# Two tiles of the last phase in two buffers each, two small tiles in another tile's buffers

## The chip, the cores and the metric

The kernel runs on one core of a Trainium2 chip. The metric is the device time of one execution in microseconds (us); lower is better. Engine names follow the profile: PE is the matmul engine, PEld its weight loads, DVE the vector engine, ACT the scalar engine, POOL GpSimd, SP the engine that issues almost all DMAs, SPq its queue.

## The reference

The program computes the forward result and all gradients of `out = x + A(LN(x)) + B(LN(x))`, with S = 2048 rows and D = 512 columns, in bf16. LN is a layer norm without weights.

```python
# A: gated long convolution
k_shift = sum_t k_pad[:, t:t+S] * shift_k[:, 3-t]        # 4 taps
kv = k_shift * v
y  = irfft(rfft(kv, 2S) * rfft(ssm_k, 2S))[:S] + kv * ssm_D
A  = xn * y                                              # xn = LN(x)
# B: bilinear GLU, F = 1376
B  = ((xn @ w_gate) * (xn @ w_up)) @ w_down
out = x + A + B
# returned: out (out_0) and the gradients for x, k, v, shift_k, ssm_k, ssm_D, w_gate, w_up, w_down
```

With `go` the gradient that comes in and `bb` the two parts that the GLU contributes to a block of rows (`x + B(xn)` and the GLU's gradient for `xn`), the element-wise end of it is, per block of rows:

```
out_0 = xn * y + bb[0]
e     = go * y ;  dxn = e + bb[1]
out_1 = go + rstd * (dxn - mean(dxn) - xn * mean(dxn * xn))     # gradient for x (the q gradient)
out_2 = four taps of (dks * shift_k), summed                     # gradient for k
```

## The kernel before

Rows are dealt as `s = 16 p + r`: partition `p` holds rows 16 p to 16 p + 15, so a tile `[128, 16, 512]` holds a whole sequence tensor, and a block `b` is the two columns of rows `2 b` and `2 b + 1`, a tile of `[128, 2, 512]` (256 KB in bf16). The FFT is done as matmuls in two stages with the spectra in DRAM in between.

The program has a first part (layer norm, FFT stages, the GLU's forward and backward pass over 8 chunks of rows) that leaves its results in DRAM scratch: `BX` (the `bb` parts), `HDD` (hidden gradients), `GD` (inverse spectra). The last phase, from about 314 us on, is where the change lies. Its main line is the generator `dw()` (weight gradients): for each of 11 blocks of the hidden dimension it loads `hb` from `HDD` (or, for the last three, `natT`, turned by the DMA), transposes it on PE (`hid_t`), multiplies it with `goC` (`down_grad`, line 1014, tile `pd`, stored by way of `od`) and with `xnC` (line 1050, tile `pu`, stored by way of `og`). At each `yield` of `dw()`, counted by `n`, a list of side generators may be advanced:

- `inv_y()`: last stage of the inverse FFT, in 8 steps. Spectra come in as `g` (line 785); the rows of `y` go to `yC`, the convolution's other gradient to tiles `dd`, from which DVE makes rows of `dks` (line 950) and `kb` (line 951, stored as out_3). For this it loads `vb` and `kb` (lines 925, 927).
- `dsk_gram()`: the gradient of `shift_k`, from `n` = 27 on. Four PSUM tiles `pk` (line 1073) are masked into `kd` (line 1079) and reduced into `dsk` (line 1081); then a transposed copy `dskt` (line 1091) is stored as out_4.
- `inv_dk()`: the gradient of `ssm_k` (tiles `po`, `o5t`).
- `ew()`: the element-wise end, one step every third `n` from `n` = 10 on. Its steps are `final(0)`, `final(1)`, `bwd(0)`, `final(2)`, `bwd(1)`, ... `final(7)`, `bwd(6)`, `bwd(7)`. `final(b)` asks for the next block's `bb` (line 1114) and computes `o` (out_0; lines 1125 and 1126) and `e` (out_1; lines 1129, 1134, 1140, 1141). `bwd(b)` computes `dk` (out_2; lines 1103 to 1106) with a helper tile `tk`. Stores are not issued where a tile is finished: they are put on a list, and `put_late()` (line 1167) issues them on SP at the start of the next step.

The order of each engine's instructions is fixed at build time. A planner goes through the traced program, and on each engine takes, of the instructions that it holds to be ready, the one traced earliest; `tc.high_priority(offset=SOON)` moves an instruction forward in that order, `tc.issue_after(ins)` keeps one behind another. On the chip every engine and SP's queue then run strictly in that order, and semaphores hold an instruction back until its inputs are there and the buffer it writes is free. A DMA that waits on SP therefore holds everything behind it on SP.

Tiles come from pools. A pool has a default number of buffers per tile name; tiles with the same `tag` share buffers. The pools of the last phase are `c2b` (two buffers: `vb`, `kb`, `dd`, `dk`, `bb`, `od`) and `c2` (one buffer: `yC`, `dks`, `o0`, `e`, `dxn`, `kd`, `dskt`, `og`, `khC` and others). In the profile `o0` appears as `o`. The hidden dimension's last `og` tile (`og1`) already sits in the buffers of `dd`. `tk` shares the one buffer of `dxn`.

Of the kernel before, what the change touches and what calls it, by code (L numbers as in the profile page):

```python
# [8 lines left out]
BF = mybir.dt.bfloat16  # L9
F32 = mybir.dt.float32  # L10
# [8 lines left out]
D = 512  # L19
F = 1376  # L20
R = 16
P = 128
NC4 = 4
# [167 lines left out]
def kernel(  # L191
# [45 lines left out]
    def dve(o, i):  # L237
        nc.vector.tensor_copy(o, i)  # L238
# [13 lines left out]
    def P2(name, shape, dt=F32):  # L252
        return ps2.tile(shape, dt, name=name, tag="p2")

    def P1(name, shape, dt=F32):
        return ps1.tile(shape, dt, name=name, tag="p1")
# [648 lines left out]
    c2b = ctx.enter_context(tc.tile_pool(name="c2b", bufs=2, side="right", reuse_waits="tile"))  # L905
    c2 = ctx.enter_context(tc.tile_pool(name="c2", bufs=1, side="right", reuse_waits="tile"))
# [160 lines left out]
    def dsk_gram():  # L1067
        for c in range(NC4):
            pk = P2("pk", [P, 2, D])
            for r in range(R):  # L1070
                for h in range(2):
                    c0 = c * 128 + 64 * h
                    nc.tensor.matmul(pk[64 * h:64 * h + 64, h, 0:256], lhsT=dks[:, r, c0:c0 + 64],  # L1073
                                     rhs=KH[0][:, r:r + 4, c0:c0 + 64], start=(r == 0), stop=(r == R - 1))
            kd = c2.tile([P, 4, 64], F32, name="kd")
            with tc.high_priority(offset=SOON):
                for h in range(2):
                    hs = slice(64 * h, 64 * h + 64)
                    nc.vector.tensor_tensor(kd[hs], pk[hs, h, 0:256].rearrange("q (j c) -> q j c", j=4),
                                            ident[hs, hs].unsqueeze(1).to_broadcast((64, 4, 64)), op=ALU.mult)  # L1080
                nc.vector.tensor_reduce(dsk[:, c, :], kd[:], axis=AX.X, op=ALU.add)
            yield
        dskb = c2.tile([P, 4, NC4], BF, name="dskb")
        nc.vector.tensor_copy(dskb[:], dsk[:].rearrange("q c i -> q i c"))
        for _ in range(2):
            yield
        pt = P1("pts", [P, 4, P], BF)
        for j in range(4):
            nc.tensor.transpose(pt[:NC4, j, :], dskb[:, 3 - j, :], ident[:])
        dskt = c2.tile([NC4, P, 4], BF, name="dskt")  # L1090
        dve(dskt[:], pt[:NC4].rearrange("c j q -> c q j"))
        nc.sync.dma_start(out_4.rearrange("(c p) j -> c p j", p=128), dskt[:])
        yield
# [18 lines left out]
    def load_fin(b):  # L1112
        bb = c2b.tile([P, 2, 2, D], BF, name="bb")
        nc.sync.dma_start(bb[:], BX[:, 2 * b:2 * b + 2, :, :])
        FL[b] = bb

    def final(b):
        if b + 1 < 8:
            load_fin(b + 1)
        bb = FL.pop(b)  # L1120
        rb = slice(2 * b, 2 * b + 2)
        tt = nc.vector.tensor_tensor
        stt = nc.vector.scalar_tensor_tensor
        o = c2.tile([P, 2, D], BF, name="o0")
        tt(o[:], xnC[:, rb], yC[:, rb], op=ALU.mult)
        tt(o[:], o[:], bb[:, :, 0, :], op=ALU.add)
        late.append((o0_n[:, rb, :], o))
        e = c2.tile([P, 2, D], BF, name="e")
        tt(e[:], goC[:, rb], yC[:, rb], op=ALU.mult)
        dxn = c2.tile([P, 2, D], F32, name="dxn")  # L1130
        for i in range(2):
            r = 2 * b + i
            stt(dxn[:, i], e[:, i], 1.0, bb[:, i, 1, :], op0=ALU.mult, op1=ALU.add, accum_out=s1[:, r:r + 1])
            stt(e[:, i], dxn[:, i], 1.0, xnC[:, r, :], op0=ALU.mult, op1=ALU.mult, accum_out=s2[:, r:r + 1])
        nc.vector.tensor_scalar(m2[:, rb], s2[:, rb], -1.0 / D, None, op0=ALU.mult)
        stt(m1[:, rb], s1[:, rb], -1.0 / D, rstd[:, rb], op0=ALU.mult, op1=ALU.mult)
        for i in range(2):
            r = 2 * b + i
            stt(dxn[:, i], xnC[:, r, :], m2[:, r:r + 1], dxn[:, i], op0=ALU.mult, op1=ALU.add)
            nc.vector.tensor_scalar(e[:, i], dxn[:, i], rstd[:, r:r + 1], m1[:, r:r + 1], op0=ALU.mult, op1=ALU.add)  # L1140
        tt(e[:], e[:], goC[:, rb], op=ALU.add)
        late.append((o1_n[:, rb, :], e))
# [16 lines left out]
    for b in range(8):  # L1159
        tail.append(lambda b=b: final(b))  # L1160
        if b > 0:
            tail.append(lambda b=b: bwd(b - 1))
# [19 lines left out]
    def load_dk():  # L1182
        gks.append(load_gk(0))
        gks.append(load_gk(1))
        yield

    sides = [every(seq(inv_y(), load_dk()), 0, 3), every(dsk_gram(), 27, 2), every(inv_dk(), 35, 3), every(ew(), 10, 3)]
    for n, _ in enumerate(dw()):
        for sd in sides:
# [36 lines left out]
```

## Time and profile before

| | us |
|---|---|
| runs (median of 3; lowest; highest) | 489.96; 488.36; 490.24 |
| the profiled execution | 488.56 |
| its span, first to last instruction | 486.8 |
| last phase: end of the last matmul | 477.08 |
| last phase: end of DVE's last instruction | 481.35 |
| DVE busy in 300 to 487 us | 113.96 of 187 |
| PE busy in 300 to 477 us | all but 0.2 |

A page of the profile gives, for one execution, the busy time of each engine, the idle time ahead of each group of instructions with what ended it, and the chain of work that ended last. In a timeline line the columns are start in us, duration in us, engine, line, operation, tiles and shape, count, and in square brackets the idle time just ahead and what released it. In the list of waits they are the total in us, the number of waits and the longest.

### The profile page before, as it was taken

The numbers are of one execution on the slowest core, as the hardware profiler recorded it, in microseconds if no ns is written. First come the engines' busy times: TensorE is split into PE (matmuls) and PEld (weight loads), VectorE is DVE, ScalarE is ACT, GpSimd is POOL, SyncE is SP. The second block draws the span as 40 slices with busy tenths as digits, with TensorE's granted clock in tenths as the row PEclk, the third lists the DMA queues.
The fourth block names the chain that finished last, engine by engine and source line by source line (L and its number), as shares of the span: only waits on it lengthen the run. The fifth ranks groups of instructions, "written<-read, shape, count | busy, mean of one in ns | idle before, by whom it ended". The sixth has DMA issues, their size and how long they took to land.

```text
span 486.8 us, 10509 instructions
## 1 busy us (share of the span) xinstructions
PE 471.5 (97%) x4335; PEld 314.8 (65%) x4335; DVE 342.0 (70%) x625; ACT 310.1 (64%) x351; POOL 13.9 (3%) x30
## 2 busy tenths in 40 slices
PE   8998999999999999999999999999999999999992
PEld 7867755547647457357357734577677778777790
DVE  7889989988275667677687874021260999998895
ACT  4956677669568678789689954567557523733320
POOL 8000000000000000000000000020000000000000
PEclk9999999999999999999999999999999999999997
DMA  8999999889999978788977199989999797999518
GB/s 266 373 366 362 314 261 359 295 314 323 306 293 284 247 235 246 240 257 250 296 231 238 63 366 324 369 314 348 342 368 373 286 354 248 316 310 231 186 48 293
DMA packets 105837, 139.87 MB, mean 287 GB/s; under 512 B 33435, under 2 KB 78912, under 8 KB 104126
## 3 DMA queue, kind: packets, MB, share of 16 engines
q1 hardware_dynamic: 104206, 137.85, 86.9%
q10 hardware_dynamic: 1584, 1.36, 1.0%
q8 instruction: 34, 0.56, 0.5%
q14 instruction: 13, 0.11, 0.1%
HBM read 68.45 MB, written 63.41 MB: 271 GB/s over the span
## 4 chain that ended last, share of the span: by engine, by line
PE 76%; DMA 11%; DVE 10%; ACT 1%; issue 1%; DVEq 0%; SPq 0%; ACTq 0%
PE px L555 14%; PE pgu L512 13%; PE pu L1050 12%; PE py L548 7%; PE pd L1014 6%; PE pdh L518 6%; PE pt L847 4%; PE pq L920 3%; PE ps L584 3%; DMA ssk<-in_A_ssm_k_dram 3%; PE pg L613 3%; PE pf L370 2%; DMA out_dram<-e 2%; DMA x_b<-in_A_q_dram 2%; PE pk L1073 2%; DMA XN<-x_b 1%
## 5 line engine op out<-in xcount | busy, mean ns | idle before, releaser
L555 PE MATMUL px<-WT,hd 128*128 128x512 bf16 (+1 forms) x352 | 81.0, 380 | 0.0
L1050 PEld LDWEIGHTS <-xnC 128*128 128x128 bf16 x704 | 67.1, 98 | 8.8 <-issue 0.9
L555 PEld LDWEIGHTS <-hd 128*128 128x128 bf16 (+1 forms) x352 | 32.8, 98 | 44.4 <-issue 7.7
L1050 PE MATMUL pu<-natd,xnC 128*128 128x256 bf16 x512 | 58.5, 273 | 0.2 <-ACT nath L235 0.2
L235 ACT CAST gu<-pgu 128x1024 bf16<-128x1024 f32 (+1 forms) x48 | 45.4, 946 | 16.5 <-PE pgu L512 16.3
L235 ACT CAST GO<-pg 128x1024 bf16<-128x1024 f32 x48 | 46.2, 1015 | 13.8 <-issue 7.2
L235 ACT CAST SP<-ps 128x1024 bf16<-128x1024 f32 x47 | 45.6, 1025 | 13.7 <-PE ps L584 11.8
L600 DVE TENSOR_TENSOR T<-SP 128x2048 bf16<-128x2048 bf16 x24 | 29.4, 1223 | 34.8 <-ACT SP L235 34.7
L512 PE MATMUL pgu<-xt,Wu 128*128 128x256 bf16 (+1 forms) x352 | 53.1, 273 | 0.7 <-DVE kn L238 0.6
L512 PE MATMUL pgu<-xt,Wg 128*128 128x256 bf16 (+1 forms) x352 | 52.8, 273 | 0.2 <-DMA Wg<-in_B_w_gate_dram 0.2
L518 PE MATMUL pdh<-gt,WdT 128*128 128x256 bf16 (+1 forms) x352 | 46.9, 273 | 0.2 <-ACT WdT L235 0.2
L235 ACT CAST fst<-pf 128x1024 bf16<-128x1024 f32 x44 | 42.7, 1030 | 5.7 <-ACT fst L235 2.1
L512 PEld LDWEIGHTS <-Wu 128*128 128x128 bf16 (+1 forms) x352 | 33.0, 100 | 15.0 <-issue 10.1
L548 PE MATMUL py<-Wd,hd 128*128 128x512 bf16 (+1 forms) x176 | 41.4, 380 | 0.0
L235 ACT COPY natd<-pt 128x2048 bf16<-128x2048 bf16 x16 | 30.0, 1874 | 14.1 <-PE pt L847 14.1
L235 ACT CAST og<-pu 128x1024 bf16<-128x1024 f32 (+1 forms) x11 | 10.9, 993 | 43.1 <-PE pu L1050 38.5
L518 PEld LDWEIGHTS <-WdT 128*128 128x128 bf16 (+1 forms) x352 | 34.8, 100 | 5.0 <-ACT WdT L235 0.4
L512 PEld LDWEIGHTS <-Wg 128*128 128x128 bf16 (+1 forms) x352 | 34.8, 100 | 4.1 <-DMA Wg<-in_B_w_gate_dram 0.5
L533 DVE TENSOR_TENSOR hd<-gu,dh 128x1024 bf16<-128x1024 bf16 (+1 forms) x48 | 30.9, 643 | 0.8
L532 DVE TENSOR_TENSOR hd<-gu 128x512 bf16<-128x512 bf16 (+1 forms) x48 | 19.1, 398 | 15.9 <-ACT gu L235 15.9
L1014 PE MATMUL pd<-goC,nath 128*128 128x512 bf16 x128 | 30.1, 379 | 0.0
L548 PEld LDWEIGHTS <-hd 128*128 128x128 bf16 (+1 forms) x176 | 16.5, 98 | 20.8 <-issue 3.1
(176 smaller groups left out, 693.2 us busy)
## 6 DMA issues: line engine op xcount, KB each, us to landing
HDD<-hd SPq DMA_DIRECT2D x35, 384.0 KB, 5.8
FD<-fst SPq DMA_DIRECT2D x24, 512.0 KB, 5.5
X<-FD SPq DMA_DIRECT2D x24, 512.0 KB, 5.2
GD<-GO SPq DMA_DIRECT2D x24, 512.0 KB, 3.9
g<-GD SPq DMA_DIRECT2D x11, 1024.0 KB, 8.7
hb<-HDD SPq DMA_DIRECT2D x8, 1344.0 KB, 7.9
bb<-BX SPq DMA_DIRECT2D x8, 512.0 KB, 6.2
BX<-bx SPq DMA_DIRECT2D x7, 512.0 KB, 3.9
```

Source lines behind the costliest of these rows:

```text
L235: nc.scalar.copy(o, i)
L512: nc.tensor.matmul(pgu[:w, i, t, :], lhsT=W[:, c, f0:f0 + w], rhs=xt[:, :, c, :], start=(c == 0), stop=(c == NC4 - 1))
L518: nc.tensor.matmul(pdh[:w, i, :], lhsT=WdT[:, c, f0:f0 + w], rhs=gt[:, :, c, :], start=(c == 0), stop=(c == NC4 - 1))
L532: nc.vector.tensor_tensor(hd[:fw, fb0:fb0 + n, 0, :], gu[:fw, :n, 0, :], gu[:fw, :n, 1, :], op=ALU.mult)
L533: nc.vector.tensor_tensor(hd[:fw, fb0:fb0 + n, 1:3, :], gu[:fw, :n], dh[:fw, :n].unsqueeze(2).to_broadcast((fw, n, 2, 256)), op=ALU.mult)
L548: nc.tensor.matmul(py[:], lhsT=hd[:fw, fb, 0, ss], rhs=Wd[:fw, fb, :], start=(fb == 0), stop=(fb == NFB - 1))
L555: nc.tensor.matmul(px[:], lhsT=hd[:fw, fb, t, ss], rhs=W[:fw, fb, :], start=(t == 1 and fb == 0), stop=(t == 2 and fb == NFB - 1))
L584: nc.tensor.matmul(ps[32 * q:32 * q + 32, a, :], lhsT=TB.EF[64 * a:64 * a + 64, 4 * g + q, ri].rearrange("p k j -> p (k j)"), rhs=X[64 * a ...
L600: tt(W[:].rearrange("p c a d -> p c (a d)"), A[:, i:i + 1].rearrange("p c a d -> p c (a d)").to_broadcast((P, 2, 2 * D)), B[:].rearrange(" ...
L847: nc.tensor.transpose(pt[:, r, :fw], hs[:, (r % 2) * 128:(r % 2) * 128 + 128], ident[:fw, :fw])
L1014: nc.tensor.matmul(pd[:fw, :], lhsT=nat_h(fb, r), rhs=goC[:, r, :], start=(r == 0), stop=(r == R - 1))
L1050: nc.tensor.matmul(pu[:, c, :, :fw], lhsT=xnC[:, r, cs(c)], rhs=nat_d(fb, r), start=(r == 0), stop=(r == R - 1))
```

## The change

`o` and `e` in `final()` get two buffers each, so that a block's tile can be written while the tile of the block before is still being stored. `kd` and `dskt` of `dsk_gram()` move from pool `c2` (one buffer each) into the two buffers of `dd` in pool `c2b`, which `inv_y()` has done with by then and `og1` takes later. No computation and no DMA is added or taken away. In bytes per partition `c2` loses 1024 for `kd` and 1024 for `dskt` and gains 2048 each for `o` and `e`; the buffers of `dd` (2048 each) keep their size.

```diff
@@ dsk_gram()
-            kd = c2.tile([P, 4, 64], F32, name="kd")
+            kd = c2b.tile([P, 4, 64], F32, name="kd", tag="dd")
...
-        dskt = c2.tile([NC4, P, 4], BF, name="dskt")
+        dskt = c2b.tile([NC4, P, 4], BF, name="dskt", tag="dd")
@@ final(b)
-        o = c2.tile([P, 2, D], BF, name="o0")
+        o = c2.tile([P, 2, D], BF, name="o0", bufs=2)
         tt(o[:], xnC[:, rb], yC[:, rb], op=ALU.mult)
         tt(o[:], o[:], bb[:, :, 0, :], op=ALU.add)
         late.append((o0_n[:, rb, :], o))
-        e = c2.tile([P, 2, D], BF, name="e")
+        e = c2.tile([P, 2, D], BF, name="e", bufs=2)
```

## The prediction

> **What bounds the kernel now.** I read the page's busy times first, then busy time by stretch for the end of the run.
>
> ```profile
> PE 471.5 (97%) x4335; PEld 314.8 (65%) x4335; DVE 342.0 (70%) x625; ACT 310.1 (64%) x351; POOL 13.9 (3%) x30
> 448.62:477.08 28.46, 28.46 (x276) 23.48 (x273) 23.77 (x50) 7.77 (x10) 0.00 (x0) 1.00 0.47 154
> 477.08:486.80 9.72, 0.01 (x1) 0.00 (x0) 4.10 (x7) 0.37 (x1) 0.00 (x0) 0.73 0.85 268
> ```
>
> The last two lines give a stretch, its length, and the busy time of PE, PEld, DVE, ACT and POOL, then PE's granted clock, DMA share and GB/s. PE has no gap up to 477.08 and nothing after it. So the end of the run is 477.08, set by PE, plus a tail of 9.7 us. The chain that ended last (start, length, what) does not run through PE there:
>
> ```profile
> 448.62 3.65 DMA out_dram<-e
> 452.27 0.02 issue
> 452.29 0.70 DVE e L1129
> ...
> 459.74 0.61 DVE e L1141
> 460.35 0.02 issue
> 460.37 4.34 DMA out_dram<-e
> 464.71 0.02 issue
> 464.74 0.69 DVE e L1129
> ```
>
> Twice the store of one block's `e` has to land before DVE may write the next block's `e`. From 452.29 to 481.35 DVE alone makes the end. The list of waits from 300 us on says how much of this there is, and the timeline where the largest falls:
>
> ```profile
> DVE o L1125 <- DMA out_dram<-o: 14.5, 1, 14.5
> DVE e L1129 <- DMA out_dram<-e: 5.1, 4, 3.3
> DVE dk L1103 <- DMA out_dram<-dk: 1.0, 2, 0.6
> 376.91 0.69 DVE L1125 TENSOR_TENSOR o<-xnC,yC 128x1024 bf16<-128x1024 bf16 x1 [14.53 <-DMA out_dram<-o]
> ```
>
> DVE stood still from 362.4 to 376.9 because the first `o` had not been stored, and worked nearly without a gap from there. The end of the run on SP and PE:
>
> ```profile
> 476.49 0.59 PE L1014 MATMUL pd<-goC,nat 128*96 128x512 bf16 x2
> 480.94 0.41 DVE L238 CAST od<-pd 96x256 bf16<-96x256 f32 x1
> 481.05 0.33 SPq L1167 DMA_DIRECT2D out_dram<-dk  x1
> 481.47 1.77 SPq L1061 DMA_DIRECT2D out_dram<-og  x2
> 483.33 0.58 SPq L1027 DMA_DIRECT2D out_dram<-od  x1
> ```
>
> PE's last result, `pd`, waits 3.9 us for DVE to finish `bwd(7)`, then its store waits 2.3 us on SP behind `dk` and the last `og`, which themselves waited for DVE. From the start of that store to the end of the span is 3.4 us (landing 2.5, closing 0.9).
>
> **The change, part by part.**
>
> *`kd` and `dskt` in the buffers of `dd`: 0.* `kd` is written and read by DVE alone. The last reads of `dd` (lines 950 and 951) end at 388.4 and the first `kd` starts at 393.3, on the same engine, so no wait can arise while that order stands. `dskt` is stored at 433.9, its buffer's next tenant `og1` is written by ACT at 473.7: 40 us of cover. If the cover were gone, the price would be one small store, 3.5 us by its landing event.
>
> *Places of the other tiles of `c2`: 0, at most 2.8.* The pool grows by 2 KB per partition, so its tiles may lie over other old tiles. The first one written, `yC`, starts at 318.6, and the one late user of the old space is the store of the last `bx`, issued at 314.05 and landed at 321.45 by its landing event. Were `yC` moved over `bx`, ACT would wait 2.8 us. I take 0, since `yC` is one of many tiles and the shift is small.
>
> *`o` in two buffers.* The multiply of `o(1)` (0.6) and, with `e`'s second buffer, that of `e(1)` (0.6) can go ahead to about 321 us, when DVE idles. The rest of `final(1)` needs `bb(1)`, issued at 354.80 and landed at 365.3. From the rows of block 1, `final` takes 384.72 − 376.91 = 7.8 us, so 6.6 remain: done at about 371.9. `bwd(0)`, whose first product is there since 329, has three products and three sums of 0.7: done at 376.1. Then `final(2)` needs the stores of `o(0)` and `e(0)` (landed 376.9 and 378.0) and `bb(2)` (landed 379.2). So what is late next is again the loads and stores on SP. By 376.9 DVE is ahead by `final(1)` and `bwd(0)`, 7.8 + 4.2 = 12.0 us. Against this, the products of line 950 then wait for `vb`, landed at 383.4 and 384.7, and may hold DVE a few us, as it runs in order. I keep 7 to 12, and take 9.
>
> *`e` in two buffers.* Takes up to 5.1 us of waits, of which 4.2 (3.3 and 0.9) lie on the chain. The first comes of a store stuck on SP behind two turning loads, `natT`, which held the queue from 436.3 to 447.9; with two buffers DVE only needs the `e` two blocks back. I take 4. With `bb(7)`, issued at 449.45 behind the same loads and landed at 453.7, `final(7)`, `bwd(6)` and `bwd(7)` still take 7.8 + 2 × 4.2 = 16.2: not before 469.9, even if nothing else is gained on that load.
>
> So DVE's last sum, at 481.0 before, comes at about 481.0 − 9 − 4 = 468 by the work, at 470 by `bb(7)`. Either is ahead of 477.08: 3.9 us would be enough. The rest of the gain is lost, since PE then ends the run.
>
> *The new tail.* PE ends at 477.08 as before; both halves of `od` are cast by 477.6 (0.37 on ACT, 0.41 on DVE). SP has `dk` and `og` behind it, as `og` was cast at 474.5 and takes 1.8 to issue. The store is issued at 477.65 and the span ends 3.4 later, at 481.1. ACT's half was issued at 478.96, 1.4 after its cast, because the semaphore it counts on was still held by a `dk` store that landed at 478.88; and it landed 3.4 after its issue. With that wait gone the end by ACT is 477.6 + 3.4 + 0.9 = 481.9, with it still there 483.3. I take 481.6, a gain of 5.2 with bounds of 3.5 and 5.7.
>
> For the store in that sum, the Trainium skill (DMA: Bandwidth & Descriptors, Anatomy of one DMA) has a fit of 2.0 us plus bytes over 436 GB/s, which makes 2.1 us for 48 KB, an estimate for another kind of queue; the rows have 2.5 and 3.4, and by the page the span would end 0.4 to 1.3 earlier than I say.
>
> Sum: 486.8 − 5.2 = 481.6 for the span, 488.56 − 5.2 = 483.4 for the profiled execution. The median of the runs lies 1.4 above that execution, so I forecast 489.96 − 5.2 = **484.8**.
>
> **The rivals.**
>
> *The gain is spent on PE or comes back on SP (no change).* Total work on PE does not shrink, and its loads have little room: by the landing events the `hb` for the sixth block (issued 366.89) landed at 382.4 and was first read at 383.87, 1.4 us to spare; the next one 1.9.
>
> ```profile
> 390.10 1.27 SPq L793 DMA_DIRECT2D hb<-HDD  x1
> 400.94 0.94 PE L847 MATMUL pt<-ident,hb 128*128 128x128 bf16 x14
> ```
>
> The stores of `o(1)` and `e(1)` would now move into 365 to 380 us, where DMAs run at their full 370 GB/s: 256 KB there is 0.7 us each, 1.4 for both. If they are queued ahead of `hb`, all its room is gone, and some us of waiting for `e(1)` come on top. A PE stall of 3 to 5 us leaves 484.8 plus that, 487.8 to 489.8. Against it: a ring that is full anyway lands `hb` by its place in the queue, and one place costs 0.7.
>
> The Trainium skill (Perfetto Trace Analysis, Identifying the Most-Contended Engine) would have the engine with the highest occupancy worked on first, here PE at 97%, and so expects nothing of shorter waits on DVE at 70%. The trace agrees up to 477 us, not for the tail, in which PE does nothing.
>
> *Stores pile up ahead of PE's loads (slower).* One mechanism: SP's order is planned anew, and stores that wait for DVE are put in front of the seventh `hb`. Its buffer is free at 382, yet it was issued at 390.10, behind a store of `e` that waited for DVE until 384.83 and two of `kb` after it. It landed at 399.0 and was read at 400.94. From an issue after 392.0 on, PE stalls one for one; the total is worse than before from 392.0 + 5.2 = 397.2 on. Were both `e(2)` and `e(3)` put in front, DVE would need another 7.8 us each, and the issue would be near 402: a stall of 10, and 489.96 + 10 − 5.2 = 494.8. For it: the order is the planner's, not known from here. Against it: DVE is earlier, not later, at each store that was in front.
>
> *The change doesn't reach the end.* If the planner puts the gained work elsewhere and DVE ends at 478 to 480, the gain is 1 to 3 us: 487 to 489.
>
> **How the numbers follow.** A measurement of this kernel can tell about 0.5% from no change, so 2.4 us. Forecast 0.72 (all of it faster, 482.5 to 487.5); no change by a short PE stall or an unfinished gain 0.14; slower 0.14. The low end is the lowest run less the largest gain, 488.36 − 5.8; the high end takes in the case of no change, to 490.0. What is left out is mainly the slower rival.
>
> **What would show it.** Right: no wait of line 1125 over 14 us; DVE's last sum of `dk` before 477; PE busy without a gap to 477; the chain ends through `pd`, `od` and its store. Wrong: PE waiting for `hb`, `natT` or `g`; a PE end later than 478; DVE still casting `od` after 479; waits of `e` replaced by waits for `bb` that end after 461.

## The result, and the profile after

| | before | after |
|---|---|---|
| runs, median (lowest to highest), us | 488.97 (486.97 to 490.24), 6 runs | 482.75 (482.32 to 483.61), 6 runs |
| the profiled execution; its span, us | 488.56; 486.8 | 482.81; 480.6 |
| end of PE's last matmul, us | 477.08 | 477.28 |
| end of DVE's last sum of `dk`, us | 481.02 | 470.55 |

The ratio of after to before is 0.9876, with a 95% interval of 0.9851 to 0.9901: faster by 1.2%. The median forecast was 484.8.

The page's busy times after, and busy time by stretch for the end (columns as before: length, PE, PEld, DVE, ACT, POOL, clock, DMA share, GB/s):

```profile
PE 471.4 (98%) x4335; PEld 314.7 (65%) x4335; DVE 341.7 (71%) x625; ACT 310.2 (65%) x351; POOL 13.9 (3%) x30
449.00:477.28 28.28, 28.28 (x274) 23.31 (x271) 16.89 (x32) 7.50 (x9) 0.00 (x0) 1.00 0.72 231
477.28:480.60 3.32, 0.00 (x0) 0.00 (x0) 0.42 (x1) 0.37 (x1) 0.00 (x0) 1.00 0.15 36
```

No engine's busy time differs by more than 0.3 us from before. In this stretch PE runs without a gap to 477.28, as it did to 477.08 before; the stretch behind it shrank from 9.72 us to 3.32. In the chain that ended last there is no DVE but for the last cast:

```profile
468.55 5.28 PE pu L1050 x64
473.82 3.47 PE pd L1014 x16
477.29 0.03 ACTq L235
477.32 0.04 issue
477.36 0.38 ACT od L235
477.74 0.02 issue
477.76 0.42 DVE od L238
```

The list of DVE's waits from 300 us on, where there were 14.5 us for the store of `o` and 5.1 for stores of `e`:

```profile
DVE o L1126 <- DMA bb<-BX: 15.8, 5, 9.1
DVE od L238 <- ACT od L235: 7.2, 1, 7.2
DVE dk L1103 <- DMA out_dram<-dk: 2.4, 1, 2.4
DVE o L1125 <- DMA out_dram<-o: 1.2, 1, 1.2
```

No wait for a store of `e` is left, and 1.2 us for one of `o`. DVE's new waits are for the loads `bb` (9.1 of the 15.8 us are for the first one, which cost 6.6 before), and 7.2 us at the end in which it has nothing to do until PE's last `pd` is there and ACT has cast its half. The loads still leave DVE's last sum 6.7 us ahead of PE's end. DVE's timeline shows what it does where it stood still, and how it ends:

```profile
366.77 0.69 DVE L1126 TENSOR_TENSOR o<-o,bb 128x1024 bf16<-128x1024 bf16 x1 [3.07 <-DMA bb<-BX]
...
376.75 0.69 DVE L1106 TENSOR_TENSOR dk<-dk,tk 128x1024 bf16<-128x1024 bf16 x1
378.62 0.69 DVE L1125 TENSOR_TENSOR o<-xnC,yC 128x1024 bf16<-128x1024 bf16 x1 [1.18 <-DMA out_dram<-o]
...
469.86 0.69 DVE L1106 TENSOR_TENSOR dk<-dk,tk 128x1024 bf16<-128x1024 bf16 x1
477.76 0.42 DVE L238 CAST od<-pd 96x256 bf16<-96x256 f32 x1 [7.20 <-ACT od L235]
```

Between 366.77 and 377.44 lie the rest of `final(1)` and the rest of `bwd(0)` (its first product was done at 329 in both kernels), work that came after 376.9 before. SP's queue at the end:

```profile
472.13 1.18 SPq L1167 DMA_DIRECT2D out_dram<-dk  x1
474.69 1.24 SPq L1061 DMA_DIRECT2D out_dram<-og  x2
478.21 0.34 SPq L1027 DMA_DIRECT2D out_dram<-od  x1
```

The last `dk` and `og` are issued before PE ends, so the store of `od` goes out 0.03 us after its cast (478.18). Where the time came from, piece by piece, between PE's end and the end of the span: the wait of the last DVE cast went from 3.86 us to 0.48, the way from that cast's end to the issue from 1.98 to 0.03, from issue to landing from 2.5 to 1.54 by the landing events, and the closing from 0.9 to 0.85. That is 6.4 us less; PE ends 0.2 later; the span is 6.2 shorter.

### The profile page after: what moved, and what is told of

It reads as the page before. It is cut to its first block, busy times and chain, and to the rows that moved or that the text cites. A ratio compares the mean times of both kernels' runs of the same rounds, so it can differ in the third digit from the quotient of the medians.

```text
span 480.6 us, 10501 instructions
## 1 busy us (share of the span) xinstructions
PE 471.4 (98%) x4335; PEld 314.7 (65%) x4335; DVE 341.7 (71%) x625; ACT 310.2 (65%) x351; POOL 13.9 (3%) x30
## 4 chain that ended last, share of the span: by engine, by line
PE 71%; DMA 15%; DVE 11%; ACT 1%; issue 1%; SPq 1%; ACTq 0%; DVEq 0%
PE px L555 15%; PE pgu L512 13%; PE pu L1050 11%; PE py L548 7%; PE pdh L518 6%; PE pd L1014 5%; PE ps L584 3%; DMA khC<-in_A_k_dram 3%; DMA ssk<-in_A_ssm_k_dram 3%; PE pg L613 3%; PE pf L370 3%; PE pt L847 2%; DMA g<-GD 2%; DMA vb<-in_A_v_dram 2%; DMA x_b<-in_A_q_dram 2%; DMA kb<-KS 2%
## 5 line engine op out<-in xcount | busy, mean ns | idle before, releaser
L512 PEld LDWEIGHTS <-Wu 128*128 128x128 bf16 (+1 forms) x352 | 33.0, 100 | 14.8 <-issue 9.8
```

The source lines that it names most:

```text
L512: nc.tensor.matmul(pgu[:w, i, t, :], lhsT=W[:, c, f0:f0 + w], rhs=xt[:, :, c, :], start=(c == 0), stop=(c == NC4 - 1))
```

## The experiments

The question was which of the two second buffers does it, whether the new places of the small tiles cost something, and what sets the end before and after.

**`o` alone** (the change, with `e` back in one buffer):

```diff
-        e = c2.tile([P, 2, D], BF, name="e", bufs=2)
+        e = c2.tile([P, 2, D], BF, name="e")
```

> The change with `e` back in one buffer (`o` in two, `kd` and `dskt` in the buffers of `dd`). By the split of the prediction (9 us of DVE's lead come from `o`, 4 from `e`), `o` alone brings DVE's last sum of `dk` from 481.0 to about 472, ahead of PE's end, so nearly the whole gain is there: about 6 us, ratio about 0.988. The rival reading: `final(1)` needs a free `e` as well as a free `o`, and the stores of `o(0)` and `e(0)` land within 1.1 us of each other (376.9 and 378.0 in the kernel before). Then the wait of 14.5 us only changes its name, to one of line 1129 on the store of `e`, the later waits of `e` stay too, and the time is within 2 us of the kernel before, ratio 0.996 to 1.000.

491.75 us (489.45 to 493.52, 12 runs) against 489.09 (23 runs): ratio 1.0053, 1.0025 to 1.0082. No gain, and half a per cent lost, which neither reading forecast. DVE's waits and its timeline at the place of the long one:

```profile
DVE o L1126 <- DMA bb<-BX: 12.4, 3, 8.5
DVE o L1125 <- DMA out_dram<-o: 11.5, 1, 11.5
DVE e L1129 <- DMA out_dram<-e: 3.8, 2, 3.4
366.07 0.69 DVE L1126 TENSOR_TENSOR o<-o,bb 128x1024 bf16<-128x1024 bf16 x1 [3.06 <-DMA bb<-BX]
378.31 0.69 DVE L1125 TENSOR_TENSOR o<-xnC,yC 128x1024 bf16<-128x1024 bf16 x1 [11.55 <-DMA out_dram<-o]
379.01 0.69 DVE L1129 TENSOR_TENSOR e<-goC,yC 128x1024 bf16<-128x1024 bf16 x1
```

Only `o(1)` moved ahead. The multiply of line 1125 that now stands still is that of `o(2)`, which the order puts in front of `e(1)`. But the place of `o(2)` costs nothing: the store of `e(0)` lands at 378.91 by its landing event, so `e(1)` at 379.01 could not have begun more than 0.1 us earlier. The stores of `o` and of `e` are issued one behind the other and land about a microsecond apart or less (0.6 us here, 1.1 in the kernel before); opening the first gate leaves DVE at the second. DVE's last sum ends at 481.57, against 481.02 before. The last sum before, then with `o` alone:

```profile
480.33 0.69 DVE L1106 TENSOR_TENSOR dk<-dk,tk 128x1024 bf16<-128x1024 bf16 x1
```

```profile
480.88 0.69 DVE L1106 TENSOR_TENSOR dk<-dk,tk 128x1024 bf16<-128x1024 bf16 x1
```

The loss shows in PE's list of waits (1.9 us for `kd`, 0.7 for `dskt`; PE ends at 479.9) and on SP, where the stores of `o5t`, `dk` and `og` follow each other without a pause up to the issue of `od` at 486.37, 3.0 later than before. That is how this profiled execution reads; no run tests it.

**`e` alone** (the change, with `o` back in one buffer):

```diff
-        o = c2.tile([P, 2, D], BF, name="o0", bufs=2)
+        o = c2.tile([P, 2, D], BF, name="o0")
```

> The change with `o` back in one buffer (`e` in two). By the split of the prediction `e` alone takes about 4 us of waits, DVE's last sum comes at about 477, close to PE's end, and the gain is 3 to 5 us, ratio 0.990 to 0.994. The rival reading, that a free `e` is what lets `final(1)` and `bwd(0)` run from 365 us on while only the two short instructions for `o(1)` wait for the store of `o(0)`: nearly all of the lead is there without `o`, DVE's last sum at 470 to 473, and the time is that of the whole change, ratio about 0.988. Either way a wait of line 1125 on the store of `o` is left, shorter than 14.5 us.

482.18 us (481.67 to 483.25, 6 runs): ratio 0.9875, 0.9849 to 0.9901, the whole gain. The timeline at the same place, and the last sum:

```profile
365.62 0.69 DVE L1133 SCALAR_TENSOR_TENSOR dxn<-e,bb 128x512 f32<-128x512 bf16 x1 [3.04 <-DMA bb<-BX]
...
374.99 0.69 DVE L1106 TENSOR_TENSOR dk<-dk,tk 128x1024 bf16<-128x1024 bf16 x1
377.29 0.69 DVE L1125 TENSOR_TENSOR o<-xnC,yC 128x1024 bf16<-128x1024 bf16 x1 [1.60 <-DMA out_dram<-o]
...
467.94 0.69 DVE L1106 TENSOR_TENSOR dk<-dk,tk 128x1024 bf16<-128x1024 bf16 x1
```

`o(1)` still waits for the store of `o(0)`, until 377.29, but the planner, which makes the order anew for each kernel, now has it behind the `e` part of `final(1)` and the rest of `bwd(0)`, and its wait is 1.60 us, not 14.53. The work behind the gate of `o` never needed `o`: nothing else reads it. The 14.53 us were put down to `o` because its multiply stood first in the queue.

What these runs leave open is which of `e`'s waits had to go. A second buffer removes all of them at once: the early one at 362 to 377 us, hidden behind that of `o`, and the two late ones on the chain (3.3 and 0.9 us). By the rows of before, the late two alone would bring the last sum from 481.0 to about 476.8, an estimate that is already just ahead of PE's end. No run frees `e` in the late blocks only.

**The places of `kd` and `dskt` alone** (both in the buffers of `dd`, `o` and `e` in one buffer):

```diff
-            kd = c2.tile([P, 4, 64], F32, name="kd")
+            kd = c2b.tile([P, 4, 64], F32, name="kd", tag="dd")
...
-        dskt = c2.tile([NC4, P, 4], BF, name="dskt")
+        dskt = c2b.tile([NC4, P, 4], BF, name="dskt", tag="dd")
```

> Only `kd` and `dskt` in the buffers of `dd`; `o` and `e` in one buffer each. The prediction costs this at 0, and takes the places of the tiles of `c2` to be without effect: same waits as before (14.5 us of line 1125, about 5 us of line 1129), ratio 0.998 to 1.002. If the tiles' places or the shared buffers did matter, it would show here alone, as a PE or ACT wait near 318 us or a wait of `kd`, and a ratio off 1 by more than 0.002.

489.22 us (486.42 to 490.85, 10 runs): ratio 1.0007, 0.9981 to 1.0033. The long waits stand as they were (14.8 us the longest for the store of `o`, 3.5 for `e`). The move costs nothing that can be measured.

**DVE's room after the change**: extra products of line 1105 in `bwd(7)`, each writing the same `tk` again, so that the results stay. The lines show six more; for twenty more the 7 is 21.

```diff
-                nc.vector.tensor_tensor(t[:], src, w, op=ALU.mult)
+                for _ in range(7 if (b, j) == (7, 3) else 1):
+                    nc.vector.tensor_tensor(t[:], src, w, op=ALU.mult)
```

Six more products:

> The whole change, and in `bwd(7)` the last product `tk` computed 7 times instead of once: 6 more DVE instructions of 0.6 to 0.7 us, some 4 us, in DVE's last stretch; the outputs stay the same. In the changed kernel DVE's last sum ends at 470.6 and PE at 477.3, so the theory (PE sets the end, DVE has 6.8 us of room) expects no change against the changed kernel: ratio to the kernel before 0.987 to 0.990, span about 480.6. The rival, that DVE still takes part in the end, by way of the `dk` store ahead of the last stores on SP, expects up to 4 us more: ratio about 0.996.

Twenty more:

> As the run before with 21 products instead of one: 20 more, 12 to 14.5 us. DVE's last sum is then due at 483 to 485, well after PE, and the theory expects the end of the kernel before to come back: `od` cast by DVE and stored on SP after `dk` and the last `og`, the span ending 4 to 6 us after the last sum, at 487 to 491. Were DVE's place off the end for another reason than its room of 6.8 us (its share of the end hidden by the stores), the span would stay below 485.

With six, 482.32 us (481.3 to 483.16, 4 runs), ratio 0.9869 (0.9819 to 0.9919): 4.3 us of added work do not show in the time. With twenty, 489.97 us (487.0 to 491.47, 8 runs), ratio 1.0013 (0.9978 to 1.0047): the old time is back. DVE's timeline with six and with twenty:

```profile
465.50 5.04 DVE L1106 TENSOR_TENSOR tk<-dks,skb 128x1024 bf16<-128x1024 bf16 x7
470.57 0.69 DVE L1107 TENSOR_TENSOR dk<-dk,tk 128x1024 bf16<-128x1024 bf16 x1
476.60 0.42 DVE L238 CAST od<-pd 96x256 bf16<-96x256 f32 x1 [5.33 <-ACT od L235]
```

```profile
469.21 15.20 DVE L1106 TENSOR_TENSOR tk<-dks,skb 128x1024 bf16<-128x1024 bf16 x21
484.45 0.69 DVE L1107 TENSOR_TENSOR dk<-dk,tk 128x1024 bf16<-128x1024 bf16 x1
485.06 0.41 DVE L238 CAST od<-pd 96x256 bf16<-96x256 f32 x1
```

With six, DVE is done at 471.26 and still waits 5.33 us before the last cast. That is only 0.7 later than without them (470.55), since `bb(7)` landed at 451.25 in this execution, 3.6 earlier than in the profiled one of the kernel after; so this trace uses up less of DVE's room than the added work suggests. With twenty it is done at 485.14, 6.3 us behind PE (478.85), and the cast waits for DVE again. DVE's end at 471.3 doesn't count and at 485.1 it does, which fits the prediction's limit, PE's end; no run places DVE's end close to it.

**Less work on PE, before and after the change**: half of the sum over rows of the last hidden block is left out of `pu` and `pd` (lines 1014 and 1050), some 4.4 us of PE at the very end, so that the weight gradients of that block are not the reference's. The lines show the loop of `pu`; that of `pd` is changed in the same way.

```diff
-                for r in range(R):
+                rf = R // 2 if last else 0
+                for r in range(rf, R):
...
```

> The kernel before with half of the sum left out in the last hidden block (8 of 16 rows in its `pd` and `pu`: 8 x 0.216 + 32 x 0.0825 = 4.4 us of PE at the very end; out_7 to out_9 are incomplete there). The theory says that DVE sets the end in this kernel, so the time stays: ratio 0.998 to 1.002, PE ending near 472.7 and the chain unchanged. If PE set the end, the time would fall by 4.4, ratio 0.991.

> The changed kernel with the same half of the last hidden block's sum left out. The theory says that PE sets the end here, so the time falls against the changed kernel: PE ends at 472.9, still after DVE's 470.6, and the span falls by 3.5 to 4.4, to 476 to 477; ratio to the kernel before 0.978 to 0.981. A smaller fall, 2 us or less, would say that the last stores on SP (`dk`, `og`, `o5t`) are the bound right behind PE.

Taken from the kernel before: 488.06 us (484.61 to 491.19, 10 runs), ratio 0.9994 (0.996 to 1.0028). Taken from the kernel after: 479.77 us (478.53 to 480.31, 4 runs), ratio 0.9808 (0.9765 to 0.985) to the kernel before. The end of PE (last `pd`) and DVE's last cast, in the one and in the other:

```profile
475.09 0.59 PE L1015 MATMUL pd<-goC,nat 128*96 128x512 bf16 x2
482.86 0.41 DVE L238 CAST od<-pd 96x256 bf16<-96x256 f32 x1
```

```profile
471.59 0.59 PE L1015 MATMUL pd<-goC,nat 128*96 128x512 bf16 x2
472.66 0.42 DVE L238 CAST od<-pd 96x256 bf16<-96x256 f32 x1 [5.48 <-ACT od L235]
```

Before, the last result of PE then lies 7 us until DVE comes to it, and the time stays. PE's end there was forecast at 472.7 and is 475.68, only 1.4 earlier than with the whole sum: its list of waits has 2.0 us for `hb` and 0.9 for `kd` in that execution. A fall of 1.4 us would be a ratio of 0.997, which the interval doesn't exclude, while a fall of 4.4 (0.991) it does. What shows that PE didn't set the end is the trace: DVE works without a marked gap from 466.65 to its last cast, which begins 7 us after PE's end. After, the cast follows 0.5 us behind PE's end and the span falls by 3.5 us (480.6 to 477.1). PE ends 5.1 us earlier there, not 4.4, in part because it waited for no `hb` in that execution (1.1 us after); 1.6 of it is lost again on SP, where `od` is issued behind two stores of `og` at 473.71, 0.63 after its cast, and lands 2.5 us after that and not 1.5. So the change has moved the end of the run from DVE to PE.

**One word**: the kernel before with only `e` in two buffers, `kd` and `dskt` where they were.

```diff
-        e = c2.tile([P, 2, D], BF, name="e")
+        e = c2.tile([P, 2, D], BF, name="e", bufs=2)
```

> The kernel before with one word changed: e in two buffers; o, kd and dskt as they were. Theory (e's gate alone stood between DVE and the path to dk, o is only an output, kd and dskt cost nothing where they are): the same as with e alone in the whole change, so a ratio of about 0.9875 to the kernel before, a span of 480.4 to 480.9, DVE's last sum of dk done at 468 to 469, PE's end at 477.0 to 477.4. Rival (the places of kd and dskt matter once DVE runs ahead, since kd would now wait for a tenant of its old buffer or the other tiles come to lie over older ones): PE waits for kd by more than 1 us and the end of PE is at 478 or later, ratio 0.990 or more.

482.11 us (481.91 to 482.88, 5 runs), against 490.11 (487.92 to 491.31, 9 runs) of the kernel before beside it: ratio 0.984, 0.9817 to 0.9864. The ratio is a little below the forecast one because the runs of before were high there; the median is that of `e` alone (482.18) and of the whole change (482.75) within 0.14%, which is no difference that can be told. The span is 480.4, DVE's last sum ends at 468.40, and the waits are those of `e` alone:

```profile
DVE o L1126 <- DMA bb<-BX: 7.5, 1, 7.5
DVE dxn L1133 <- DMA bb<-BX: 4.0, 3, 2.8
DVE dk L1103 <- DMA out_dram<-dk: 2.5, 1, 2.5
DVE o L1125 <- DMA out_dram<-o: 1.4, 1, 1.4
```

The second buffer of `e` is what the change is worth; that of `o`, and the room made for it, bring nothing that these runs can tell.

## Why the prediction was right, and where it was not

*What bounds the kernel: right.* DVE's lateness made the tail behind PE. Taking work from PE did nothing that could be measured before the change and shortened the run after it. Two readings there are loose: DVE doesn't make the end alone from 452.29 on, since the chain shown there holds another store of `e`, 4.34 us long, up to 464.71; and the store of `od` waits 1.98 us on SP from the end of DVE's cast (481.35 to 483.33), not 2.3.

*`kd`, `dskt` and the places in `c2` at 0: right.* The moves alone gave a ratio of 1.0007.

***`o` worth 9 us, `e` worth 4: wrong.*** This is the step that failed. `o` alone moved DVE's last sum by 0.55 us in the wrong direction (481.02 to 481.57), `e` alone moved it by 12.4 in the right one (468.63). The split was a mistake in reading. The time was forecast well in spite of it, because the time can't tell a lead of 4 us from one of 13: with more than 3.9 us PE ends the run, and `e` alone and the whole change take the same time. That the sum of the two terms, 13, lies near what was measured, 12.4 with `e` alone and 10.5 with the whole change, is in part luck, as in both runs the load `bb(7)` was the bound and not the leads. The list of waits names the instruction at the head of the queue, and I gave the 14.5 us to its tile. The prediction's own working held the warning: its account of what could run ahead under `o` used "`e`'s second buffer" and had the two stores land about a microsecond apart (376.9 and 378.0). Of these two gates, which open nearly together, the one that the later work doesn't need is worth nothing, whatever the wait is called, and the other is worth the whole gain. The one that was needed was `e`: `dxn` is computed from it, and `tk` of `bwd` shares the buffer of `dxn`, while `o` is read by nothing but its own second step (line 1126) and its store.

*DVE's end at 468 by the work, at 470 by `bb(7)`: right.* It was 470.55, and the load was the bound: `bb(7)` landed at 454.88 (forecast from 453.7) and `final(7)`, `bwd(6)` and `bwd(7)` took 15.7 us behind it. With `e` alone the same load landed at 452.28 and the end was 468.6. DVE's wait for `bb(7)` in the kernel after:

```profile
454.91 0.69 DVE L1126 TENSOR_TENSOR o<-o,bb 128x1024 bf16<-128x1024 bf16 x1 [1.74 <-DMA bb<-BX]
```

*PE's end unchanged: right within 0.2 us.* The rival's concern was real but small, and one of the prediction's signs of being wrong, PE waiting for `hb`, did appear: the `hb` for the sixth block landed at 383.68, 1.3 later than before, which used up its room of 1.4.

```profile
PEld L847 <- DMA hb<-HDD: 0.8, 1, 0.8
PE pt L847 <- DMA hb<-HDD: 0.3, 1, 0.3
```

The stores of `o(1)` and `e(1)` were issued on SP behind this `hb`, at 379.66 and 380.49, not in front. The next `hb` was issued at 391.34, short of the 392.0 from which a rival had PE stall, and landed at 399.07, as before (399.0).

*The end of the span, 481.6: mis-sized by 1.0.* Two terms were off in opposite directions. I let both halves of `od` be cast at once, by 477.6; DVE's half began only when ACT's was done, so its store was issued at 478.21, 0.56 later. And I kept the 2.5 and 3.4 us from issue to landing of before; they were 1.54 on SP and 1.63 on ACT. At that time the queues had nothing else to carry but the last of `dk` and `og`, which landed at 478.25 to 479.22; that this is the cause was not tested. ACT's store did not wait: it was issued at 477.76, right behind its cast. The Trainium skill (DMA: Bandwidth & Descriptors, Anatomy of one DMA) with its fit for another kind of queue gave 2.1 us for this store, an estimate; its direction against the rows of before was right, and the measured 1.54 lies below it too.

Between the profiled executions the gain was 5.75 us (488.56 to 482.81) where the spans give 6.2, and between the medians 6.2. So the median of 482.75 lies 2.0 below the 484.8 forecast for two reasons of about the same size: the gain was 1.0 larger, and the kernel before had a median of 488.97 over six runs, not the 489.96 from which the forecast started.

## What to carry to other kernels

When an in-order engine waits long for a buffer, look past the instruction that waits: ask what stands behind it, which tile that work needs, and when that tile's own gate opens. Of two gates that open together, give the second buffer to the tile that the later work needs, which may not be the one named in the list of waits; and try each buffer alone before paying for room for both. An engine at 70% can set the end of a run if it is late by a few microseconds at the very end, and the gain from hurrying it stops where the busiest engine ends.

## What was not expected of the hardware

- The two casts of the two halves of one PSUM tile `pd` ran one behind the other, ACT's from 477.36 and DVE's from 477.76 in the kernel after, and likewise in each other kernel in which DVE was free at PE's end. The profile names the ACT cast as what released DVE's; whether the engines or the order written by the build cause this was not tried.
- Issue to landing of the same 48 KB store on SP was 1.54 to 1.55 us where SP had issued nothing for 2 us ahead of it (after, `e` alone, six more products), and 1.96 to 2.54 with two stores of `og` issued just ahead of it (1.96 with twenty more products, 2.5 before).
- The runs of kernels that end with PE lie closer together (482.32 to 483.61 after, 481.91 to 482.88 with `e` alone in one line) than those of kernels that end with DVE (486.59 to 491.91 in the 23 runs of before beside `o` alone). The cause was not sought.
